# One-query attention over 8192 keys: VectorE turns the outputs for 64-byte stores, TensorE takes the value sum of two heads back first, and scores and softmax of a head run in one go

## The chip, the core and the metric

The kernel runs on one core of one Trainium2 chip. The metric is the device time of one execution in microseconds (us); the median of three runs of the kernel before is 326.26 us (326.13 to 326.35). A profile of one more execution, with the time of every instruction and DMA, stands beside it.

A core has five engines that run side by side and meet at semaphores: TensorE (PE in the profile; its weight loads are PEld), VectorE (DVE), ScalarE (ACT), GpSimd (POOL) and SyncE (SP). Here SP only issues DMAs; ACT issues three. A DMA issue is carried out in the order in which its engine comes to it, after the waits that stand ahead of it.

## What is computed

```python
B, H, Sq, Sk, D = 1, 16, 1, 8192, 256          # q, k, v in bf16
def reference(q, k, v):
    scale = q.shape[-1] ** -0.5
    scores = jnp.einsum("bhqd,bhkd->bhqk", q, k) * scale
    p = _softmax(scores, axis=-1)
    return jnp.einsum("bhqk,bhkd->bhqd", p, v)
```

For each of 16 heads one query row of 256 numbers meets 8192 keys, and the softmax of the 8192 scores weighs 8192 rows of values. A head's keys are 4 MB (4096 KB in the profile's rows) and so are its values: 134.2 MB in all, each byte used once. The output is 16 rows of 256 bf16 numbers, 8 KB.

## The kernel before

**Layout.** Partition p holds keys 64p to 64p+63 of a head, so a block of 64 keys of 256 numbers lies in each of the 128 partitions (`kbuf`, `vbuf`; two buffers of each, for even and odd heads). J is 64, the number of keys in a partition; j counts them.

**One head h** goes through these steps.

1. *Scores.* VectorE takes 48 of the 64 keys of each partition: 48 multiply-and-sum instructions (L189), each of which leaves one column of `S`. TensorE takes the other 16 (`NPE`), in four groups (`NG`) of four keys: it transposes a group (L292), ScalarE copies the transposed group from PSUM to `KT` (L392), and TensorE multiplies it with the query (L306). ScalarE then copies the 16 columns into `S` (L396, semaphore `sc`), and the last of VectorE's 48 instructions waits for that copy (L188). VectorE's last instruction raises `kd`.
2. *Maximum.* VectorE takes the maximum of `S` along each partition (L205, `m`), TensorE turns that column into a row (L226), VectorE takes its maximum (L171, `xmax`, result `g`), and TensorE spreads it over the partitions (L232, `bcast`).
3. *Exponentials.* ScalarE negates the maximum (L400) and takes the exponentials into `E`, with sums along each partition (L404). TensorE adds the sums up (L242, `total`), and VectorE takes the reciprocal (L176, `recips`).
4. *Value sum* (`pv`, L258). TensorE runs 128 matmuls of one column: the weights are a 128x128 block of `vbuf`, the moving column is one of `E`. Output number 2p+f of the head comes to partition p, column f (f is 0 or 1), because the weights are every second column of `vbuf`. ScalarE scales the two columns with the reciprocal into `o_col` (L416, `final`).

**Order on TensorE.** A loop over i has nine turns; turn i works on heads 2i and 2i+1, and on the value sums of heads 2i-2 and 2i-1. Written out for turn i: scores of 2i; value sum of 2i-2, and between its matmuls the maximum's turn (after 32 of 64 keys), the spreading (after 48) and the total (after 64) of head 2i-1; the maximum's turn of 2i, scores of 2i+1 with the spreading of 2i after the second group; value sum of 2i-1; total of 2i. Turn 0 has no value sums, turn 8 no scores; branches skip those parts.

**Order of the loads.** SP issues them from a list. From head 2 on it is: keys of h+2, values of h. Keys of h+2 wait for `kd` of head h (VectorE is done with the buffer), values of h wait for `pv` of head h-2. SP stands at each wait, so a late one holds back everything behind it. The values of head 14 come in two halves and those of head 15 in five pieces (`V_LATE`: from keys 0, 28, 46, 56 and 61), each with a semaphore of its own, so that TensorE can begin head 15's sum before its last piece is there.

**The end.** The outputs of heads 0 to 14 lie in `o_col`, 128 partitions by 30 columns. When TensorE is 46 keys into head 15's sum, it turns them with two matmuls against an identity (L274) into 15 rows of 256; ScalarE copies these to `o_row` (L470) and stores them in one DMA of 15 runs of 512 bytes (L472). Head 15's two columns are scaled by ScalarE (L416) and stored as they lie: 128 runs of 4 bytes (L475). ScalarE waits for both stores.

Of the kernel before, what the change touches and what calls it, by code (L numbers as in the profile page):

```python
# [14 lines left out]
V_LATE = {14: (0, 32), 15: (0, 28, 46, 56, 61)}  # L15
# [24 lines left out]
def bass_standalone__mha_softmax__decode_kernel(nc: bass.Bass, q: bass.AP, k: bass.AP, v: bass.AP, out: bass.AP):  # L40
# [28 lines left out]
    with contextlib.ExitStack() as ctx:  # L69
# [31 lines left out]
        o_col = sb("o_col", [P, H * NH], out.dtype)  # L101
        o_row = sb("o_row", [H - 1, D], out.dtype)
# [10 lines left out]
        for name in ("l", "rc", "pv", "fin", "ldq", "k0", "k0a", "k0b", "k1", "va0", "va1", "tr", "cp", "o"):  # L113
            sem(name)
# [8 lines left out]
        if True:  # L123

            @(lambda f: f(nc.sync))
            def _(sp):
                for kind, h, a, b, name in stream:
                    buf = (kbuf if kind == "k" else vbuf)[h % 2]
                    if h >= 2 and a == 0:
                        if kind == "k":  # L130
                            sp.wait_ge(sem("kd"), h)
                        else:
                            sp.wait_ge(sem("pv"), h + 1)
                    sp.dma_start(  # L134
                        buf[:, a * D : b * D], src(k if kind == "k" else v, h)[:, a * D : b * D]
                    ).then_inc(sem(name), 16)
                sp.nop()

            @(lambda f: f(nc.gpsimd))
            def _(pool):  # L140
# [18 lines left out]
                pool.memset(ones_row[:, :], 1.0).then_inc(sem("cf"), 1)  # L159
                pool.memset(ones_col[:, :], 1.0).then_inc(sem("cf"), 1)  # L160
# [7 lines left out]
            def _(dve):  # L168
# [37 lines left out]

                with dve.Fori(0, H // 2) as i:  # L207
# [12 lines left out]
                recips(last)  # L220

            @(lambda f: f(nc.tensor))
            def _(pe):
# [26 lines left out]
                def pv(h, waits, at):  # L250
# [3 lines left out]
                    for j in range(J):  # L254
                        for name, value in waits.get(j, ()):
                            pe.wait_ge(sem(name), value)
                        for hf in range(NH):
                            ins = pe.matmul(  # L258
                                acc[h.par][:, hf : hf + 1],
                                lhsT=vbuf[h.par][:, j * D + hf : (j + 1) * D : NH],  # L260
# [7 lines left out]
                        if j + 1 in at:  # L268
                            at[j + 1]()

                def rows():
                    pe.wait_ge(sem("fin"), H + 3)
                    for hf in range(NH):
                        ins = pe.matmul(  # L274
                            spe[0 : H - 1, hf : D : NH],
                            lhsT=o_col[:, hf : (H - 1) * NH : NH],
                            rhs=identb[:, :],
                            start=True,
                            stop=True,
                        )  # L280
                    ins.then_inc(sem("tr"), 1)
# [33 lines left out]
                def scores(t, before=None):  # L315
                    if before:
                        transpose_m(before)
                    for gi in range(NG):
                        ktrans(t, gi)
                        if gi >= 1:  # L320
                            kscore(t, gi - 1)
                        if gi == 1 and before:
                            bcast(before)
                    kscore(t, NG - 1)

# [31 lines left out]
                pe.wait_ge(sem("cf"), 4)  # L357
                with pe.Fori(0, H // 2 + 1) as i:
                    ev, od = _Step(0, i), _Step(1, i)
                    fin_turn = pe.snap((i // 8) * 16 + 16)  # L360
                    old = od.back(2)
                    with pe.If(i < H // 2):
                        scores(ev)
                    with pe.If(i > 0):
                        pv(
                            ev.back(2),
                            {V_LATE[14][n]: [(V_SEMS[0][n], fin_turn)] for n in range(1, len(V_SEMS[0]))},
                            {32: lambda: transpose_m(old), 48: lambda: bcast(old), 64: lambda: total(old)},
                        )
                    with pe.If(i < H // 2):  # L370
                        scores(od, before=ev)
                    with pe.If(i > 0):
                        waits = {V_LATE[15][n]: [(V_SEMS[1][n], fin_turn)] for n in range(1, len(V_SEMS[1]))}


                        def at_end():
                            with pe.If(i == H // 2):
                                rows()

                        pv(old, waits, {V_LATE[15][2]: at_end})  # L380
                    with pe.If(i < H // 2):
                        total(ev)

            @(lambda f: f(nc.scalar))
            def _(act):
# [58 lines left out]
                act.wait_ge(sem("cf"), 4)  # L444
                with act.Fori(0, H // 2) as i:
                    for c in (0, 1):
                        t = _Step(c, i)
                        for gi in range(NG):
                            evac(t, gi)
                        if c:  # L450
                            expo(t.back(1))
                        scopy(t)
                        act.wait_ge(sem("kd"), t.of(1, 1))
                        q_copy(_Step(c + 1, i), q_all[:, bass.ds(i * (2 * QW) + (c + 1) * QW, QW)])
                        with act.If(i > 0):
                            if c == 0:
                                expo(t.back(1))
                            else:
                                for d in (0, 1):
                                    at = nc.s_assert_within(  # L460
                                        (i - 1) * (2 * NH) + d * NH,
                                        0,
                                        (H - 1) * NH,
                                        skip_runtime_bounds_check_because="the branch is taken from turn 1 on",
                                    )
                                    final(t.back(3 - d), o_col[:, bass.ds(at, NH)])
                expo(_Step(H - 1))
# [4 lines left out]
                act.dma_start(out[0, 0 : H - 1, 0, :], o_row[:, :]).then_inc(sem("o"), 16)  # L472
                final(_Step(H - 1), o_col[:, (H - 1) * NH : H * NH])
                act.wait_ge(sem("fin"), H + 4)
                act.dma_start(  # L475
                    out[0, H - 1, 0, :].rearrange("(p f) -> p f", f=NH), o_col[:, (H - 1) * NH : H * NH]
                ).then_inc(sem("o"), 16)
                act.wait_ge(sem("o"), 32)
# [29 lines left out]
```

## Time and profile before

| | us |
|---|---|
| median of three runs | 326.26 |
| the profiled execution, its own time | 326.59 |
| span of its profile, first instruction to last | 325.1 |
| PE busy (3189 matmuls) | 168.6 |
| PEld busy | 143.9 |
| DVE busy | 274.8 |
| ACT busy | 91.1 |
| POOL busy | 1.6 |

The span leaves out 1.49 us of the profiled execution's own time. Busy times overlap and need not add up to the span. In a row of the timeline the columns are: start, duration, engine and line, operation, tiles written <- read, shapes, number of instructions merged into the row, and in brackets the idle time of the engine before it and what ended it. SPq and ACTq are issues of DMAs. In the list of waits the columns are: who waited, for whom, us in total, how often, the longest. In the list of DMA issues the last column is the time from the issue to the landing.

### The profile page before, as it was taken

To read this page: it belongs to the slowest core of one execution; us is meant where nothing else is said; L and a number is where in the kernel's file an instruction comes from. 1 tells how busy PE (TensorE), PEld (TensorE's weight loads), DVE (VectorE), ACT (ScalarE), POOL (GpSimd) and SP (SyncE) were. 2 spreads that over 40 slices of the span, in tenths; PEclk is the share of its full clock that TensorE was granted. 3 is DMA by queue.
4 is the path that set the end of the run, shared out by engine and by line. 5 is a ranking of instruction groups with operands and counts; after the bars stand their busy time and mean duration, and the time that the engine had idled before them with its cause. 6 is when DMAs were issued, how large, how long until landed. Compare 5 with 4: busy or idle time off the path is not lost.

```text
span 325.1 us, 8819 instructions
## 1 busy us (share of the span) xinstructions
PE 168.6 (52%) x3189; PEld 143.9 (44%) x3189; DVE 274.8 (85%) x1584; ACT 91.1 (28%) x173; POOL 1.6 (0%) x11
## 2 busy tenths in 40 slices
PE   4427280856467247643456454554646525675560
PEld 1326260755357235543335443444545424555550
DVE  3998999999999998897979979798897979979400
ACT  5435140425024140512306041250503305042010
POOL 1000000000000000000000000000000000000000
DMA  8999999999999999999999999999999999999970
GB/s 317 455 397 441 413 458 411 395 423 431 439 435 423 439 431 431 427 439 431 427 435 435 423 439 427 431 431 431 435 427 435 435 423 435 435 427 413 428 304 0
DMA packets 6116, 134.31 MB, mean 413 GB/s; under 512 B 831, under 2 KB 990, under 8 KB 1246
## 3 DMA queue, kind: packets, MB, share of 16 engines
q1 hardware_dynamic: 5904, 134.22, 96.5%
q8 instruction: 3, 0.05, 0.1%
q10 hardware_dynamic: 206, 0.02, 0.0%
q14 instruction: 3, 0.02, 0.0%
HBM read 134.23 MB, written 0.01 MB: 413 GB/s over the span
## 4 chain that ended last, share of the span: by engine, by line
DVE 50%; DMA 42%; issue 3%; PE 1%; SPq 1%; DVEq 0%; ACT 0%; ACTq 0%
DVE kbuf L189 47%; DMA kbuf<-in_k_dram 28%; DMA vbuf<-in_v_dram 14%; DVE S L189 2%; PE acc L258 1%; SPq L134 1%; DVE g L171 1%; DVE recip L176 0%; PE mx L226 0%; DVE m L205 0%; DVEq L181 0%; ACT o_col L416 0%; DVEq L207 0%; DVEq L180 0%; ACTq L415 0%
## 5 line engine op out<-in xcount | busy, mean ns | idle before, releaser
L189 DVE CUSTOM_DVE_ANT_0 kbuf<-kbuf,q_now 128x256 bf16<-128x256 bf16 x768 | 268.6, 414 | 28.4 <-DMA kbuf<-in_k_dram 27.4
L392 ACT ACTIVATE KT<-tp 128x1024 bf16<-128x1024 bf16 x64 | 63.8, 1022 | 98.6 <-PE tp L292 97.9
L292 PE MATMUL tp<-identb,kbuf 128*128 128x128 bf16 x512 | 62.8, 310 | 49.1 <-DMA kbuf<-in_k_dram 49.1
L258 PE MATMUL acc<-E,vbuf 128*128 128x1 bf16 x2048 | 60.4, 165 | 44.1 <-DMA vbuf<-in_v_dram 43.9
L258 PEld LDWEIGHTS acc<-E,vbuf 128*128 128x128 bf16 x2048 | 57.4, 104 | 49.6 <-DMA vbuf<-in_v_dram 46.2
L292 PEld LDWEIGHTS tp<-identb,kbuf 128*128 128x128 bf16 x512 | 50.7, 142 | 54.0 <-DMA kbuf<-in_k_dram 48.2
L189 DVE DVE_READ_ACCUMULATOR2_ANT S<- 128x1 f32 x768 | 58.8, 77 | 0.0
L306 PE MATMUL spe<-q_now,KT 128*128 128x1 bf16 x512 | 24.3, 169 | 16.7 <-ACT KT L392 15.9
L306 PEld LDWEIGHTS spe<-q_now,KT 128*128 128x128 bf16 x512 | 20.7, 108 | 26.4 <-ACT KT L392 21.6
L400 ACT ACTIVATE negb<-sm 128x1 f32<-128x1 f32 x16 | 2.7, 168 | 73.8 <-PE sm L232 73.8
L232 PE MATMUL sm<-g,ones_row 1*128 1x1 f32 x32 | 9.3, 356 | 21.3 <-DVE g L171 21.3
L232 PEld LDWEIGHTS sm<-g,ones_row 1*128 1x128 f32 x32 | 7.9, 304 | 22.0 <-DVE g L171 21.9
L226 PE MATMUL mx<-ident,m 128*1 128x128 f32 x32 | 9.4, 396 | 12.1 <-issue 6.2
L416 ACT ACTIVATE o_col<-acc,recip 128x2 f32 (+1 forms) x16 | 4.1, 254 | 39.8 <-PE acc L258 39.8
L242 PE MATMUL qps<-lsum,ones_col 128*128 128x1 f32 x32 | 9.1, 352 | 0.3 <-ACT E L404 0.3
L242 PEld LDWEIGHTS qps<-lsum,ones_col 128*128 128x128 f32 x32 | 8.0, 311 | 0.4 <-ACT E L404 0.4
L226 PEld LDWEIGHTS mx<-ident,m 128*1 128x1 f32 x32 | 1.4, 81 | 13.0 <-DVE m L205 6.6
L387 ACT ACTIVATE q_now<-q_all 128x258 bf16 x16 | 6.7, 418 | 0.1
L176 DVE RECIPROCAL recip<-qps 128x1 f32<-128x1 f32 x16 | 2.6, 165 | 4.2 <-PE qps L242 4.2
L171 DVE TENSOR_REDUCE g<-mx 1x1 f32<-1x128 f32 x16 | 4.4, 275 | 1.7 <-PE mx L226 1.7
L404 ACT ACTIVATE E<-S,negb 128x64 bf16<-128x64 f32 x16 | 5.6, 348 | 0.5
L348 PE MATMUL acc<-q_sb,identb 16*128 16x256 bf16 x16 | 4.3, 404 | 0.8 <-ACT q_all L439 0.8
(27 smaller groups left out, 21.1 us busy)
## 6 DMA issues: line engine op xcount, KB each, us to landing
kbuf<-in_k_dram SPq DMA_DIRECT2D x15, 4096.0 KB, 21.7
vbuf<-in_v_dram SPq DMA_DIRECT2D x12, 4096.0 KB, 31.1
vbuf<-in_v_dram SPq DMA_DIRECT2D x6, 2048.0 KB, 21.9
kbuf<-in_k_dram SPq DMA_DIRECT2D x2, 1024.0 KB, 5.9
kbuf<-in_k_dram SPq DMA_DIRECT2D x1, 2048.0 KB, 11.4
vbuf<-in_v_dram SPq DMA_DIRECT2D x1, 1792.0 KB, 10.4
vbuf<-in_v_dram SPq DMA_DIRECT2D x1, 1152.0 KB, 12.9
vbuf<-in_v_dram SPq DMA_DIRECT2D x1, 640.0 KB, 14.0
```

The costliest lines, as they stand in the source:

```text
L171: dve.tensor_reduce(g[0:1, h.par : h.par + 1], mx[0:1, 0:P], AX.X, ALU.max).then_inc(sem("g"), 1)
L189: ins = dve.tensor_tensor_reduce(out=buf[:, j * D : (j + 1) * D], in0=buf[:, j * D : (j + 1) * D], in1=q_now[h.par][:, 0:D], scale=SCALE, ...
L226: pe.matmul(mx[0:1, 0:P], lhsT=m[:, h.par : h.par + 1], rhs=ident[:, :], start=True, stop=True).then_inc(sem("mT"), 1)
L232: pe.matmul(sm[:, 0:1], lhsT=ones_row[0:1, 0:P], rhs=g[0:1, h.par : h.par + 1], start=True, stop=True,).then_inc(sem("bc"), 1)
L242: pe.matmul(qps[:, 0:1], lhsT=ones_col[:, 0:1].to_broadcast([P, P]), rhs=lsum[:, h.par : h.par + 1], start=True, stop=True,).then_inc(sem( ...
L258: ins = pe.matmul(acc[h.par][:, hf : hf + 1], lhsT=vbuf[h.par][:, j * D + hf : (j + 1) * D : NH], rhs=E[h.par][:, j : j + 1], start=(j == ...
L292: ins = pe.transpose(tp[gi % 2][:, b * D + hf * P : b * D + (hf + 1) * P], buf[:, j * D + hf * P : j * D + (hf + 1) * P], identb[:, :],)
L306: ins = pe.matmul(spe[:, c : c + 1], lhsT=KT[gi % 2][:, b * D + hf * P : b * D + (hf + 1) * P], rhs=q_now[h.par][:, D + hf : D + hf + 1], ...
L348: ins = pe.matmul(acc[pair % 2][:, (h % 2) * D : (h % 2 + 1) * D], lhsT=identb[0:H, h : h + 1].to_broadcast([H, P]), rhs=q_sb[:, :], start ...
L387: act.activation(out=q_now[h.par][:, :], in_=src_q, func=ACT.Copy).then_inc(sem("qb"), 1)
L392: act.activation(out=KT[gi % 2][:, :], in_=tp[gi % 2][:, :], func=ACT.Copy).then_inc(sem("kt"), 1)
L404: act.activation(out=E[h.par][:, :], in_=S[h.par][:, :], func=ACT.Exp, bias=negb[:, h.par : h.par + 1], scale=1.0, accum_out=lsum[:, h.par ...
```

## The change

Four things are changed together.

**Order on TensorE and ScalarE.** Turn i is now, for c = 0 and 1: value sum of head 2i-2+c, then scores of head 2i+c with the maximum's turn, the spreading and the total of the same head right behind them. ScalarE's part of a head follows suit: scaling of head t-2's output, the next query, the four copies, the copy into `S`, the exponentials of head t itself. On VectorE `xmax` of a head comes after the fourth, and `recips` after the twenty-first instruction of the next head, for even and odd heads alike.

**The values of head 14** come in one DMA, not in two halves.

**Column layout of the outputs.** The weights of the value sum are 128 neighbouring columns of `vbuf`, not every second: output number 128f+p comes to partition p, column f.

**Turning and storing.** TensorE's two turning matmuls and ScalarE's copy are gone. VectorE transposes `o_col` (128x32) in blocks of 32x32 into `o_row`, and ScalarE stores heads 0 to 14 in four DMAs, each of 30 runs of 64 bytes. Head 15's columns are scaled by VectorE into `z_col` (128x64, zeroed by GpSimd at the start, one live column in each block of 32), transposed into `z_row`, and stored by SP, which has issued all loads by then: 8 runs of 64 bytes. SP waits for all five stores. VectorE, TensorE and ScalarE wait at their start until GpSimd's two added memsets are done as well (`cf` reaches 6, not 4).

```diff
-V_LATE = {14: (0, 32), 15: (0, 28, 46, 56, 61)}
+V_LATE = {15: (0, 28, 46, 56, 61)}
+BLK = 32
...
+                sp.wait_ge(sem("tr"), 2)
+                sp.dma_start(
+                    out[0, H - 1, 0, :].rearrange("(f b x) -> b f x", f=NH, x=BLK),
+                    z_row[0:P:BLK, :].rearrange("b (f x) -> b f x", f=NH),
+                ).then_inc(sem("o"), 16)
+                sp.wait_ge(sem("o"), 16 * (P // BLK + 1))
...
-                    head(ev, {2: lambda: later(recips, ev.back(2)), 40: lambda: later(xmax, prev)})
-                    head(od, {2: lambda: later(recips, prev), 3: lambda: xmax(ev)})
+                    head(ev, {3: lambda: later(xmax, prev), 20: lambda: later(recips, prev)})
+                    head(od, {3: lambda: xmax(ev), 20: lambda: recips(ev)})
                 last = _Step(H - 1)
-                recips(last.back(1))
                 xmax(last)
                 recips(last)
+                dve.wait_ge(sem("fin"), H + 3)
+                dve.transpose(o_row[:, :], o_col[:, :]).then_inc(sem("tr"), 1)
+                dve.wait_ge(sem("rc"), last.of(1, 3))
+                dve.wait_ge(sem("pv"), last.of(1, 3))
+                dve.tensor_scalar(
+                    out=z_col[:, 0 : NH * BLK : BLK],
+                    in0=acc[last.par][:, 0:NH],
+                    scalar1=recip[:, last.par : last.par + 1],
...
+                dve.transpose(z_row[:, :], z_col[:, :]).then_inc(sem("tr"), 1)
...
-                                lhsT=vbuf[h.par][:, j * D + hf : (j + 1) * D : NH],
+                                lhsT=vbuf[h.par][:, j * D + hf * P : j * D + (hf + 1) * P],
...
+                def scores(t):
                     for gi in range(NG):
                         ktrans(t, gi)
                         if gi >= 1:
                             kscore(t, gi - 1)
                     kscore(t, NG - 1)
+                    transpose_m(t)
+                    bcast(t)
+                    total(t)
...
+                    for c, waits in (
+                        (0, {HALF: [(V_SEMS[0][1], 16)]}),
+                        (1, {V_LATE[15][n]: [(V_SEMS[1][n], fin_turn)] for n in range(1, len(V_SEMS[1]))}),
+                    ):
+                        with pe.If(i > 0):
+                            pv(_Step(c, i).back(2), waits)
+                        with pe.If(i < H // 2):
+                            scores(_Step(c, i))
...
                 final(_Step(H - 2), o_col[:, (H - 2) * NH : (H - 1) * NH])
                 act.wait_ge(sem("tr"), 1)
-                act.activation(out=o_row[:, :], in_=spe[0 : H - 1, 0:D], func=ACT.Copy).then_inc(sem("cp"), 1)
-                act.wait_ge(sem("cp"), 1)
-                act.dma_start(out[0, 0 : H - 1, 0, :], o_row[:, :]).then_inc(sem("o"), 16)
-                final(_Step(H - 1), o_col[:, (H - 1) * NH : H * NH])
-                act.wait_ge(sem("fin"), H + 4)
-                act.dma_start(
-                    out[0, H - 1, 0, :].rearrange("(p f) -> p f", f=NH), o_col[:, (H - 1) * NH : H * NH]
-                ).then_inc(sem("o"), 16)
-                act.wait_ge(sem("o"), 32)
+                rows = out.rearrange("b h s (f e) -> (b h s f) e", f=NH)
+                for b in range(0, P, BLK):
+                    act.dma_start(
+                        rows[0 : (H - 1) * NH, b : b + BLK], o_row[b : b + (H - 1) * NH, :]
+                    ).then_inc(sem("o"), 16)
```

On TensorE, before, this is the middle of a turn: after the scores of the even head 2i the skip of turn 0 (L364), the value sum of 2i-2 (L258), and between its matmuls the softmax steps of the odd head before (`mx` the maximum's turn, `sm` the spreading, `qps` the total).

```order
L364 COMPARE_AND_BRANCH
L252 ISA
L253 ISA
L258 MATMUL acc<-E,vbuf 128x1 x64
L226 MATMUL mx<-ident,m 1x128
L256 ISA
L258 MATMUL acc<-E,vbuf 128x1 x32
L232 MATMUL sm<-g,ones_row 128x1
L258 MATMUL acc<-E,vbuf 128x1 x32
L241 REGISTER_ALU
L242 MATMUL qps<-lsum,ones_col 128x1
```

On TensorE, after the change, the same place: the last score matmuls of the even head, its three softmax steps, and then the value sum of the odd head before.

```order
L316 MATMUL spe<-q_now,KT 128x1 x8
L249 REGISTER_ALU
L250 MATMUL mx<-ident,m 1x128
L256 MATMUL sm<-g,ones_row 128x1
L265 REGISTER_ALU
L266 MATMUL qps<-lsum,ones_col 128x1
L375 UNCONDITIONAL_BRANCH
L373 COMPARE_AND_BRANCH
L276 ISA
L277 ISA
L282 MATMUL acc<-E,vbuf 128x1 x56
```

The softmax steps have moved out of the value sum and stand, all three, between a head's scores and the value sum of the head before it; the scores of the next head come behind that value sum.

On ScalarE, before, this is the program's end: after the loop the exponentials of head 15, the scaling of head 14, the copy of the turned rows with their store, and the scaling and store of head 15.

```order
L445 COMPARE_AND_BRANCH
L400 ACTIVATE negb<-sm 128x1
L404 ACTIVATE E,lsum<-S,negb 128x64
L416 ACTIVATE o_col<-acc,recip 128x2
L470 ACTIVATE o_row<-spe 15x256
L472 DMA out_dram<-o_row 15x256
L416 ACTIVATE o_col<-acc,recip 128x2
L475 DMA out_dram<-o_col 128x2
```

On ScalarE, after the change, the last steps of the loop (copy into `S`, then the exponentials of the same head), its branch, and the program's end.

```order
L390 ACTIVATE S<-spe 128x16
L393 REGISTER_ALU
L394 ACTIVATE negb<-sm 128x1
L398 ACTIVATE E,lsum<-S,negb 128x64
L439 REGISTER_ALU
L439 COMPARE_AND_BRANCH
L410 ACTIVATE o_col<-acc,recip 128x2
L460 DMA out_dram<-o_row 30x32 x4
```

The exponentials have moved into the head's own step, the copy to `o_row` is gone, one store has become four, and head 15's scaling and store have left ScalarE for VectorE and SP.

More of the change, by code (lines that the diff above doesn't have):

```diff
@@ L267, in pv @@
                             ins.then_inc(sem("pv"), 1)
[L268 to L281, printed above, removed]
                 def ktrans(h, gi):
@@ L448, in _ @@
+                        q_copy(_Step(c + 1, i), q_all[:, bass.ds(i * (2 * QW) + (c + 1) * QW, QW)])
                         for gi in range(NG):
                             evac(t, gi)
-                        if c:
-                            expo(t.back(1))
                         scopy(t)
[L453 to L466, printed above, removed]
```

57 lines of the change are left out of this document (25 added, 32 removed).

## The prediction, made before the changed kernel was run

> **What bounds the kernel now.** I read the page first, then the windows (us; busy time of each engine; granted clock, DMA share, GB/s), then whom SP, the issuer of the loads, waits for.
>
> ```profile
> span 325.1 us, 8819 instructions
> PE 168.6 (52%) x3189; PEld 143.9 (44%) x3189; DVE 274.8 (85%) x1584; ACT 91.1 (28%) x173; POOL 1.6 (0%) x11
> DMA  8999999999999999999999999999999999999970
> ...
> 151.00:190.00 39.00, 20.52 (x399) 17.90 (x399) 34.45 (x199) 10.55 (x20) 0.00 (x0) 1.00 1.00 432
> ...
> SPq L134 <- DVE S L189: 250.0, 14, 19.2
> SPq L134 <- PE acc L258: 33.4, 2, 17.6
> ```
>
> The DMA engines are busy from the first slice to the last but one; in the middle their share is 1.00. The last slice (317 to 325 us) is empty of DMA and, as the end below shows, of everything else. SP waits for VectorE, but that costs nothing while the queue is full. So 314 us are loading, and the last 8 are something else. One turn in the middle:
>
> ```profile
> 167.89 0.33 SPq L134 DMA_DIRECT2D kbuf<-in_k_dram  x1
> ...
> 170.38 1.89 PE L292 MATMUL tp<-identb,kbuf 128*128 128x128 bf16 x16 [1.62 <-DMA kbuf<-in_k_dram]
> ...
> 180.10 3.58 PE L258 MATMUL acc<-E,vbuf 128*128 128x1 bf16 x128 [3.16 <-DMA vbuf<-in_v_dram]
> ...
> 187.46 0.33 SPq L134 DMA_DIRECT2D kbuf<-in_k_dram  x1
> ...
> 189.81 1.89 PE L292 MATMUL tp<-identb,kbuf 128*128 128x128 bf16 x16 [5.71 <-DMA kbuf<-in_k_dram]
> ```
>
> Keys land at 170.38, values at 180.10, the next keys at 189.81: 9.7 us for 4 MB, 19.43 us a head. VectorE needs 274.8/16 = 17.2 us a head, so the loads set the pace. The end:
>
> ```profile
> 296.67 3.57 PE L258 MATMUL acc<-E,vbuf 128*128 128x1 bf16 x128 [3.15 <-DMA vbuf<-in_v_dram]
> ...
> 306.47 1.01 PE L258 MATMUL acc<-E,vbuf 128*128 128x1 bf16 x32 [1.56 <-DMA vbuf<-in_v_dram]
> ...
> 308.80 0.57 PE L242 MATMUL qps<-lsum,ones_col 128*128 128x1 f32 x2
> ...
> 310.77 1.65 PE L258 MATMUL acc<-E,vbuf 128*128 128x1 bf16 x56 [1.40 <-DMA vbuf<-in_v_dram]
> 313.55 1.12 PE L258 MATMUL acc<-E,vbuf 128*128 128x1 bf16 x36 [1.13 <-DMA vbuf<-in_v_dram]
> ...
> 315.12 1.59 PE L258 MATMUL acc<-E,vbuf 128*128 128x1 bf16 x36
> ...
> 315.63 0.58 ACTq L472 DMA_DIRECT2D out_dram<-o_row  x1
> 316.81 0.26 ACT L416 ACTIVATE o_col<-acc,recip 128x2 bf16<-128x2 f32 x1 [1.21 <-PE acc L258]
> 317.10 0.37 ACTq L475 DMA_DIRECT2D out_dram<-o_col  x1
> ...
> out_dram<-o_row ACTq DMA_DIRECT2D x1, 7.5 KB, 1.3
> out_dram<-o_col ACTq DMA_DIRECT2D x1, 0.5 KB, 8.0
> ```
>
> TensorE follows the last pieces of values as they land and is done at 315.12 + 1.59 = 316.71. The store of 15 runs of 512 bytes lands in 1.3 us, that of 128 runs of 4 bytes in 8.0 us: 317.10 + 8.0 is the span's end. A fifteenth of the bytes takes six times as long, so runs, not bytes, are paid for.
>
> **The new order in the middle: cost nothing.** The value sum now stands ahead of the next head's scores. Values of t-2 land 9.7 us after keys of t, so the scores of t start later than now, and VectorE's last instruction waits for them. The length of the scores, from the one place where they run alone:
>
> ```profile
> 39.02 1.89 PE L292 MATMUL tp<-identb,kbuf 128*128 128x128 bf16 x16 [5.67 <-DMA kbuf<-in_k_dram]
> ...
> 44.68 0.38 PE L306 MATMUL spe<-q_now,KT 128*128 128x1 bf16 x8 [0.69 <-ACT KT L392]
> ...
> 45.09 0.18 ACT L396 ACTIVATE S<-spe 128x16 f32<-128x16 f32 x1 [0.47 <-PE spe L306]
> ```
>
> 45.09 + 0.18 - 39.02 = 6.25 us, ScalarE's copies within. In the quoted turn: values land at 180.1, sum to 183.7, scores to 189.9, VectorE's last instruction some 0.4, then SP issues the next keys at 190.4 instead of 187.46. Behind SP's wait stand those keys and the values after them. The queue holds until the values in flight land, 180.1 + 19.43 = 199.5. Less 1.3 us to get going (an estimate: the small store's whole time) that leaves a margin of 7.8 us. This is the cover; once the chain is longer, every us costs about one per head. VectorE idles up to 3 us more a head and works just behind the landing instead of ahead of it. The value wait of SP (`pv`) is met at 183.7, before the key wait: nothing. The loop kd, softmax (3.6, below), sum 3.6, scores 6.25, last instruction 0.4 is 13.9 us, under 19.4, so it doesn't bind either.
>
> **The new order at the end: +1.0 us.** Scores of head 15 now wait for the value sum of 13 (ends 296.67 + 3.57 = 300.24), and both remaining sums wait for head 15's softmax. Its steps, from VectorE's last instruction of a head:
>
> ```profile
> 303.60 0.41 DVE L189 CUSTOM_DVE_ANT_0 kbuf<-kbuf,q_now 128x256 bf16<-128x256 bf16 x1
> ...
> 304.32 0.58 PE L226 MATMUL mx<-ident,m 128*1 128x128 f32 x2 [0.89 <-DVE m L205]
> 304.95 0.28 DVE L171 TENSOR_REDUCE g<-mx 1x1 f32<-1x128 f32 x1 [0.49 <-PE mx L226]
> ...
> 56.45 0.27 DVE L171 TENSOR_REDUCE g<-mx 1x1 f32<-1x128 f32 x1
> 56.78 0.58 PE L232 MATMUL sm<-g,ones_row 1*128 1x1 f32 x2 [8.44 <-DVE g L171]
> ...
> 58.17 0.57 PE L242 MATMUL qps<-lsum,ones_col 128*128 128x1 f32 x2
> ```
>
> Scores end at 300.24 + 6.25 = 306.5; now the last instruction starts at 303.60. To the start of L171 1.35, to the spreading 0.33, to the total 1.39, the total 0.57: 310.1. With 0.2 for the loop's branch the sum of 14 runs from 310.3 (its values landed at 306.47, so that their coming in one DMA costs nothing) to 313.9. With 0.2 for the skipped scores, the sum of 15 runs from 314.1 to 317.7; the pieces land ahead of it (the second at 313.5, the rest by 316.4, now's end less the six last matmuls). 317.7 instead of 316.71. Bounds: 0 (the data's own limit) to +1.8, because of the weights, now neighbouring columns:
>
> ```profile
> L258 PE MATMUL acc<-E,vbuf 128*128 128x1 bf16 x2048 | 60.4, 165 | 44.1 <-DMA vbuf<-in_v_dram 43.9
> ...
> L306 PE MATMUL spe<-q_now,KT 128*128 128x1 bf16 x512 | 24.3, 169 | 16.7 <-ACT KT L392 15.9
> ```
>
> L306 loads such weights already: eight in 0.38 us, (380 - 169)/7 = 30 ns apart, against (3580 - 165)/127 = 27 ns for L258. I take the same 27; at 30 the two sums are 0.8 longer.
>
> **The end itself: -6.3 us.** VectorE's scaling follows the last matmul by 0.1, as ScalarE's does now: 317.8. The trace has no VectorE scaling or transpose of this kind; the nearest row is the 0.28 of L171, bounds 0.1 and 0.5 each; I take 0.28 twice and a hand-over: issue by SP at 318.45 instead of 317.10. Its 8 runs of 64 bytes land in 1.3 us at best (o_row) and 8.0 at worst (o_col). I take 1.3, since 8 runs are nearer to 15 than to 128. End 319.8, so **-5.3 us** with the 1.0 from above (317.10 + 8.0 = 325.1 against 318.45 + 1.3). The four row stores start once VectorE has turned heads 0 to 14, 313.9 + 0.1 + 0.26 + 0.28 = 314.6; four issues of 0.58 (L472) put the last at 316.3, landed by 317.7: beside the last sum. The removed turning matmuls and copy lay in front of 315.63, off the path: nothing. GpSimd's two memsets come on top of 1.6 us for eleven instructions:
>
> ```profile
> 5.65 0.42 DVE L189 CUSTOM_DVE_ANT_0 kbuf<-kbuf,q_now 128x256 bf16<-128x256 bf16 x1 [5.65 <-DMA kbuf<-in_k_dram]
> ...
> 8.06 1.09 PE L348 MATMUL acc<-q_sb,identb 16*128 16x256 bf16 x4 [0.20 <-ACT q_all L439]
> 13.13 1.87 PE L292 MATMUL tp<-identb,kbuf 128*128 128x128 bf16 x16 [3.98 <-DMA kbuf<-in_k_dram]
> ...
> 22.36 0.33 SPq L134 DMA_DIRECT2D kbuf<-in_k_dram  x1
> ...
> 25.34 0.59 PE L226 MATMUL mx<-ident,m 128*1 128x128 f32 x2 [6.20 <-issue]
> ```
>
> VectorE waits until 5.65 for keys anyway: nothing. TensorE's first skip over a value sum cost 6.20 us in which it waited for nothing shown. Now that skip comes at 9.2, before the scores of head 0: they start at 15.4 instead of 13.13 and end at 21.7, just before VectorE's last instruction (22.36 less 0.4). Nothing, by 0.3 us.
>
> **Rivals.** *Small stores are paid by the run.* (8.0 - 1.3)/128 = 52 ns a run; 120 row runs take 6.3 us: 314.6 + 1.3 + 6.3 + 0.4 for the last eight = 322.6, **323.8** as a measured time. For it: o_col. Against: its runs shared 512 bytes, sixteen runs to each 64, while no two of the new ones share 64 bytes. The Trainium skill, DMA: Bandwidth & Descriptors, section Specifications, puts the line at 512 B: below it the engine reads, modifies and writes. By that rule 64 bytes fare like 4, and the time is this rival's; the 1.3 of the 512-byte runs agrees with the rule, and nothing here shows 64.
>
> *The last store is slow whatever its runs.* If what takes 8.0 us is a store's landing after the loads, not its runs, the end is 318.45 + 8.0 = 326.5, **327.6**, slower. It decides from a landing of 7.3 us on (8.0, less the later issue of 1.35, plus 0.65 or 0.2%). Against: o_row's 1.3, taken while the last loads landed.
>
> *The queue runs dry early.* VectorE begins heads late at first:
>
> ```profile
> 59.17 0.33 SPq L134 DMA_DIRECT2D kbuf<-in_k_dram  x1
> ...
> 73.25 1.89 PE L292 MATMUL tp<-identb,kbuf 128*128 128x128 bf16 x16 [2.74 <-DMA kbuf<-in_k_dram]
> ```
>
> Keys issued at 59.17 landed at 73.25; their transfer began by 63.5, so issue may slip to 62.2. The first visit of each value sum may cost 6.2 us like the skip. Head 1 leaves VectorE at 22.4 + 17.2 = 39.6; softmax 3.6, stall 6.2, sum 3.6, scores 6.25 and 0.4 put the issue at 59.7. It holds by 2.5; a second stall in the scores, and the same for head 3, would cost 1 to 3 us: **322 to 324**.
>
> *Skips cost 6.2 us in the last turn too.* The one between the last two sums would put the end at 325.8: **327.0**. Against: the same skip now lies between 308.80 + 0.57 = 309.4 and 310.77, where values landed; so it takes 1.4 us at most. The Trainium skill, Runtime: NRT & Kernel Launch, section Instruction fetch mechanics, says that a taken branch out of the fetched window waits for a fetch; turn 0 agrees, the last turn does not.
>
> **How the numbers follow.** The profiled execution took 326.59, 1.49 beyond its span; the median is 326.26, so I take the difference from the median: 326.26 - 5.3 = 320.9. Chances: forecast 0.64 (its own range 319.8 to 322.3: tail 0 to 1.8, VectorE's two steps, landing to 2.0), runs 0.12, dry queue 0.10, slow last store 0.09, skips 0.05. The range reaches over the first three, 319.8 to 324.2. These are faster by over 0.2% (0.65 us, about what a measurement can tell): 0.86. Of the other 0.14, 0.04 fall within 0.2% and 0.10 beyond.
>
> **What would show it.** SP's issue of keys some 3 us later in each turn, DMA share still 1.00 in the middle; TensorE done near 317.7; the row stores landed before the last issue; o_col's 8.0 replaced by under 2. It is wrong if a window before 300 us has a DMA share under 1.00, or a 64-byte store takes over 3 us.

## The result and the profile after

The changed kernel took 320.96 us (median of four runs, 320.66 to 321.17), beside 326.31 us for the kernel before on the same chip (four runs, 326.13 to 326.6). The ratio is 0.9835, with a 95% interval of 0.9818 to 0.9852: 5.3 us faster, as forecast (320.9). The profiled execution took 321.17, 1.27 beyond its span.

The page after, first its busy times, then its slices of DMA:

```profile
span 319.9 us, 8825 instructions
...
PE 166.6 (52%) x3187; PEld 141.6 (44%) x3187; DVE 276.0 (86%) x1587; ACT 91.8 (29%) x171; POOL 1.7 (1%) x13
...
DMA  8999999999999999999999999999999999999993
```

The work is the same, and so is the loading: only the empty time behind the last loads is gone. The last slice is shorter and no longer empty. The window of one turn in the middle (us, length, busy time of PE, PEld, DVE, ACT and POOL, granted clock, DMA share, GB/s), and whom SP waits for:

```profile
151.00:190.00 39.00, 20.23 (x396) 17.51 (x396) 34.46 (x199) 10.81 (x21) 0.00 (x0) 1.00 1.00 432
```

```profile
SPq L137 <- DVE S L200: 253.7, 14, 18.9
SPq L137 <- PE acc L282: 31.1, 2, 19.1
SPq L141 <- DVE z_row L244: 15.5, 1, 15.5
SPq L146 <- DMA out_dram<-z_row: 1.0, 1, 1.0
```

The DMA share is 1.00 at 432 GB/s, both as before. SP still waits most for VectorE. The last line, 1.0 us for the landing of head 15, and the 0.68 us of its issue, below, are what the 8.0 of `o_col` has become. The timeline of a turn:

```profile
180.26 3.57 PE L282 MATMUL acc<-E,vbuf 128*128 128x1 bf16 x128 [5.50 <-DMA vbuf<-in_v_dram]
...
183.70 1.87 PE L302 MATMUL tp<-identb,kbuf 128*128 128x128 bf16 x16
...
189.95 0.43 DVE L200 CUSTOM_DVE_ANT_0 kbuf<-kbuf,q_now 128x256 bf16<-128x256 bf16 x1 [2.21 <-ACT S L390]
...
190.41 0.33 SPq L137 DMA_DIRECT2D kbuf<-in_k_dram  x1
...
194.15 0.59 PE L266 MATMUL qps<-lsum,ones_col 128*128 128x1 f32 x2 [0.73 <-ACT E L398]
```

The values still land at 180.26 (180.10 before), their sum now stands in front of the scores, VectorE's last instruction has the new wait of 2.21 us, and SP issues the next keys at 190.41 where it had issued them at 187.46. The timeline of the end:

```profile
296.84 3.57 PE L282 MATMUL acc<-E,vbuf 128*128 128x1 bf16 x128 [5.51 <-DMA vbuf<-in_v_dram]
...
306.32 0.18 ACT L390 ACTIVATE S<-spe 128x16 f32<-128x16 f32 x1 [0.47 <-PE spe L316]
...
309.55 0.58 PE L266 MATMUL qps<-lsum,ones_col 128*128 128x1 f32 x2 [0.73 <-ACT E L398]
...
310.36 7.13 PE L282 MATMUL acc<-E,vbuf 128*128 128x1 bf16 x256 [0.23 <-issue]
...
314.33 0.21 DVE L233 STREAM_TRANSPOSE o_row<-o_col 128x32 bf16<-128x32 bf16 x1 [3.99 <-ACT o_col L410]
314.57 1.85 ACTq L460 DMA_DIRECT2D out_dram<-o_row  x4
317.61 0.23 DVE L236 TENSOR_SCALAR z_col<-acc,recip 128x2 bf16<-128x2 f32 x1 [3.07 <-PE acc L282]
317.87 0.25 DVE L244 STREAM_TRANSPOSE z_row<-z_col 128x64 bf16<-128x64 bf16 x1
318.15 0.68 SPq L141 DMA_DIRECT2D out_dram<-z_row  x1
```

TensorE no longer stops for pieces of values: the sums of heads 14 and 15 are one row of 256 matmuls without a gap, done at 310.36 + 7.13 = 317.49 (316.71 before). From there it is 0.66 us to the last issue, and 0.68 + 1.0 from that to its landing: 319.83, the span's end.

### The profile page after: what moved, and what is told of

The parts are those of the page before. It is cut to its first block, busy times and chain, and to the rows that moved or that the text cites. A ratio compares the mean times of both kernels' runs of the same rounds, so it can differ in the third digit from the quotient of the medians.

```text
span 319.9 us, 8825 instructions
## 1 busy us (share of the span) xinstructions
PE 166.6 (52%) x3187; PEld 141.6 (44%) x3187; DVE 276.0 (86%) x1587; ACT 91.8 (29%) x171; POOL 1.7 (1%) x13
## 4 chain that ended last, share of the span: by engine, by line
DMA 59%; PE 18%; DVE 12%; ACT 5%; issue 4%; SPq 1%; DVEq 0%; ACTq 0%
DMA vbuf<-in_v_dram 52%; DVE kbuf L200 11%; PE acc L282 9%; DMA kbuf<-in_k_dram 7%; PE tp L302 6%; ACT KT L386 5%; PE spe L316 2%; SPq L137 1%; ACT S L390 0%; DVE S L200 0%; PE sm L256 0%; PE qps L266 0%; DVE g L182 0%; PE mx L250 0%; ACT E L398 0%
## 5 line engine op out<-in xcount | busy, mean ns | idle before, releaser
L200 DVE CUSTOM_DVE_ANT_0 kbuf<-kbuf,q_now 128x256 bf16<-128x256 bf16 x768 | 269.4, 410 | 31.8 <-ACT S L390 21.2
L282 PE MATMUL acc<-E,vbuf 128*128 128x1 bf16 x2048 | 57.1, 166 | 60.4 <-DMA vbuf<-in_v_dram 60.0
L282 PEld LDWEIGHTS acc<-E,vbuf 128*128 128x128 bf16 x2048 | 56.0, 104 | 61.7 <-DMA vbuf<-in_v_dram 61.0
L200 DVE DVE_READ_ACCUMULATOR2_ANT S<- 128x1 f32 x768 | 55.8, 73 | 0.0
L390 ACT ACTIVATE S<-spe 128x16 f32<-128x16 f32 x16 | 2.9, 183 | 7.5 <-PE spe L316 7.5
## 6 DMA issues: line engine op xcount, KB each, us to landing
vbuf<-in_v_dram SPq DMA_DIRECT2D x1, 640.0 KB, 13.9
```

The lines of the kernel that those rows point to most:

```text
L200: ins = dve.tensor_tensor_reduce(out=buf[:, j * D : (j + 1) * D], in0=buf[:, j * D : (j + 1) * D], in1=q_now[h.par][:, 0:D], scale=SCALE, ...
L282: ins = pe.matmul(acc[h.par][:, hf : hf + 1], lhsT=vbuf[h.par][:, j * D + hf * P : j * D + (hf + 1) * P], rhs=E[h.par][:, j : j + 1], star ...
```

## The experiments

Two questions were to be told apart. How much of the 5.3 us is the end, and what does the new order cost? And why is the old last store slow: is it paid by its 128 runs, by their crowding in 512 bytes, or because it is the last? Eleven kernels ran, in three groups, each beside the kernel before (326.25, 326.7 and 326.28 us).

| kernel | us (median) | ratio to before, interval |
|---|---|---|
| after, again | 320.95 | 0.9835 [0.9822, 0.9849] |
| old order, new end | 320.61 | 0.9822 [0.9809, 0.9835] |
| old order, last head's store alone new | 320.48 | 0.9817 [0.9804, 0.9831] |
| new order, old end | 327.26 | 1.0028 [1.0019, 1.0037] |
| 60 idle transposes a head | 321.86 | 0.9863 [0.9838, 0.9888] |
| last store on two queues | 320.75 | 0.9831 [0.9818, 0.9845] |

The five others are single runs, and are read by a landing or by far larger differences. Between profiles of one kernel the loads land some tenths sooner or later (the sum of head 13 begins at 296.84 in one profile of the changed kernel and at 296.59 in that of its second run here), so the ends of two profiles are compared from a landing that both have: this sum begins as its values land, at 296.67 in the profile before and at 296.84 after. From there TensorE is done after 20.04 us before (316.71) and after 20.65 in the changed kernel (317.49).

**The changed kernel again**, as the reference for the others of its group:

> The changed kernel once more, beside the other three of this call: 320.96 as measured, within 0.3.

It took 320.95 (320.71 to 321.02).

**The old order with the new end.** The hunks of the change for weights, turning and stores on the kernel before; its order and the halves of head 14 stay. Against the kernel after, on TensorE:

```diff
-                        with pe.If(i > 0):
-                            pv(_Step(c, i).back(2), waits)
-                        with pe.If(i < H // 2):
-                            scores(_Step(c, i))
+                    with pe.If(i < H // 2):
+                        scores(ev)
+                    with pe.If(i > 0):
+                        pv(ev.back(2), ..., {32: lambda: transpose_m(old), 48: lambda: bcast(old), 64: lambda: total(old)})
+                    with pe.If(i < H // 2):
+                        scores(od, before=ev)
+                    with pe.If(i > 0):
+                        pv(old, waits, {})
+                    with pe.If(i < H // 2):
+                        total(ev)
```

> The orders of before on TensorE, ScalarE and VectorE and the two halves of head 14's values, with the new column layout, turning and stores. Theory (the stores bring the gain, the order costs about 1 at the end and nothing in the middle): TensorE is done at 316.7 as before, SP issues the last store 0.7 later, it lands 1.7 after that as it does in the changed kernel: span 319.1, time 320.2 to 320.4, that is 0.6 to 0.9 below the changed kernel. Rival (the new order brings part of the gain): the time lies above the changed kernel's 321.

It took 320.61 (320.3 to 320.76). The timeline of its end:

```profile
296.93 3.57 PE L283 MATMUL acc<-E,vbuf 128*128 128x1 bf16 x128 [3.16 <-DMA vbuf<-in_v_dram]
...
315.43 1.57 PE L283 MATMUL acc<-E,vbuf 128*128 128x1 bf16 x36 [0.48 <-DMA vbuf<-in_v_dram]
...
317.12 0.23 DVE L237 TENSOR_SCALAR z_col<-acc,recip 128x2 bf16<-128x2 f32 x1 [7.19 <-PE acc L283]
...
317.66 0.68 SPq L141 DMA_DIRECT2D out_dram<-z_row  x1
```

The new end by itself gives 326.25 - 320.61 = 5.6 us, all of the gain and 0.3 more. The new order costs that 0.3 (320.95 - 320.61); the intervals overlap, so by the medians its sign is shown only together with the kernel that has the old end, below. The expectation was lower (a larger cost of the order). In this profile TensorE waits for values until 315.43 and is done at 317.00, 0.3 later than the kernel before (316.71) with the same order, because the loads land that much later in it: the sum of head 13 begins at 296.93, and 20.07 us pass from there, as before (20.04). Against the 20.65 of the changed kernel the order costs 0.6 us by the profiles. Why loads land later in one profile than in another was not settled.

**The old order, and only the last head's store new.** As the one before, but heads 0 to 14 are turned by TensorE, copied by ScalarE and stored in one DMA of 512-byte runs:

```diff
-                rows = out.rearrange("b h s (f e) -> (b h s f) e", f=NH)
-                for b in range(0, P, BLK):
-                    act.dma_start(
-                        rows[0 : (H - 1) * NH, b : b + BLK], o_row[b : b + (H - 1) * NH, :]
-                    ).then_inc(sem("o"), 16)
+                act.activation(out=o_row[:, :], in_=spe[0 : H - 1, 0:D], func=ACT.Copy).then_inc(sem("cp"), 1)
+                act.wait_ge(sem("cp"), 1)
+                act.dma_start(out[0, 0 : H - 1, 0, :], o_row[:, :]).then_inc(sem("o"), 16)
```

> As the run before, but heads 0 to 14 are turned by TensorE, copied by ScalarE and stored in one DMA of 512-byte runs, as in the kernel before; only head 15 goes through VectorE and SP. Theory (the row stores are beside the value sum, only the last store counts): the same time as the run before within 0.3, 320.2 to 320.5. Rival (the row stores' 120 runs of 64 bytes hold the last store up): 0.5 or more below the run before.

It took 320.48 (320.03 to 320.78): not told apart from 320.61. The four row stores with their 120 runs of 64 bytes lie beside the path, and the whole gain is in how head 15 is turned and stored.

**The new order with the old end.** The order of the change; weights, turning matmuls, copy and stores of the kernel before:

```diff
-                            pv(_Step(c, i).back(2), waits)
+                            pv(_Step(c, i).back(2), waits, {V_LATE[15][2]: at_end} if c else {})
...
+                act.dma_start(
+                    out[0, H - 1, 0, :].rearrange("(p f) -> p f", f=NH), o_col[:, (H - 1) * NH : H * NH]
+                ).then_inc(sem("o"), 16)
```

> The new orders on the engines and head 14's values in one DMA, with the column layout, the turning on TensorE and the two stores of before. Theory (the order costs 0.8 to 1.4 at the end, the two turning matmuls now lying inside the last sum, and nothing else): 327.1 to 327.7, slower than before. Rival (the order saves time in the middle): at or below the 326.3 of before.

It took 327.26 (326.63 to 327.78, eleven runs), 1.0 us more than before, and the interval of the ratio lies above 1. The timeline of its end, and its list of DMA issues (last column: us from issue to landing):

```profile
296.56 3.58 PE L258 MATMUL acc<-E,vbuf 128*128 128x1 bf16 x128 [5.52 <-DMA vbuf<-in_v_dram]
...
310.04 6.17 PE L258 MATMUL acc<-E,vbuf 128*128 128x1 bf16 x220 [0.18 <-issue]
316.14 0.59 PE L274 MATMUL spe<-identb,o_col 128*15 128x128 bf16 x2
316.66 1.12 PE L258 MATMUL acc<-E,vbuf 128*128 128x1 bf16 x36
317.88 0.26 ACT L404 ACTIVATE o_col<-acc,recip 128x2 bf16<-128x2 f32 x1 [0.74 <-PE acc L258]
318.17 0.36 ACTq L457 DMA_DIRECT2D out_dram<-o_col  x1
```

```profile
out_dram<-o_col ACTq DMA_DIRECT2D x1, 0.5 KB, 8.1
```

Alone, the new order is a loss. From the start of the sum of head 13 TensorE is done after 21.2 us (317.78 - 296.56), 1.2 more than before. Of that 0.5 is the two turning matmuls (from 316.14 to 316.66): in the old order they fell into a wait for values, here they stand in a sum that waits for nothing. The rest, 0.7, is about the 0.6 that the order costs with the new end, which takes these matmuls out. By the medians the order is worth +1.0 with the old end and +0.3 with the new one, and the new end is worth -5.6 in the old order and -6.3 (327.26 - 320.95) in the new one.

**Idle transposes in front of the scores**, in turns 2 to 6, to make SP's issue of the keys later and see where the cover ends (60 and 110 of them, the count in the third line):

```diff
+                        with pe.If(i > 1):
+                            with pe.If(i < H // 2 - 1):
+                                for _ in range(60):
+                                    pe.transpose(tp[0][:, 0:P], identb[:, :], identb[:, :])
                         with pe.If(i < H // 2):
                             scores(_Step(c, i))
```

> The changed kernel with 60 idle transposes (some 5.8 us) between value sum and scores in turns 2 to 6, heads 4 to 13. SP issues keys 10.3 us after values land; with the pad 16.1, against 18.1 at which the queue would run dry by my estimate. Theory (a margin of 7.8 us covers the new order): no change, 321 within 0.5, SP's issues 5.8 us later. Rival (the margin is used up or smaller than 5 us): each of ten heads pays up to 5.8 us, 330 to 380.

With 60 it took 321.86 (321.45 to 322.61). The timeline of one head, and a window of four heads' loads:

```profile
183.20 5.60 PE L378 MATMUL tp<-identb 128*128 128x128 bf16 x60
...
194.35 0.33 SPq L137 DMA_DIRECT2D kbuf<-in_k_dram  x1
```

```profile
120.00:200.00 80.00, 57.38 (x1064) 52.08 (x1065) 70.76 (x409) 21.07 (x40) 0.00 (x0) 0.67 1.01 432
```

From the end of the value sum to SP's issue of keys it is 194.35 - 183.20 = 11.15 us, in the changed kernel 190.41 - 183.70 = 6.71. The keys come 4.4 later, and the loads still run at 432 GB/s. The time is 0.9 above the changed kernel's, a little more than the 0.5 that was allowed (0.5 when each is held against the kernel before in its own group, and the intervals of the ratios overlap); had each of the ten padded heads passed on the 4.4, it would be 44. The loads are not late in this profile: the sum of head 13 begins at 296.33, in the changed kernel at 296.84. What is late is the end: the sum of head 14 begins at 310.59, 0.2 later, and 0.4 pass between it and that of head 15, where the changed kernel has no gap. So of the margin of 7.8 us that was forecast to be left, some 4 at least are there.

> The same with 110 (some 10.7 us): 21.0 us after the landing, 2.9 over the margin, ten heads: about 350 by the theory, between 340 and 360. Rival (the issue of the keys isn't what the queue waits for): 321 as without.

With 110 it took 342.86, inside what the theory gave, but for another reason. Its timeline of one head, and the same window:

```profile
208.16 0.33 SPq L137 DMA_DIRECT2D kbuf<-in_k_dram  x1
...
212.69 3.57 PE L282 MATMUL acc<-E,vbuf 128*128 128x1 bf16 x128 [0.21 <-issue]
216.13 7.75 PE L378 MATMUL tp<-identb 128*128 128x128 bf16 x110
...
229.44 0.33 SPq L137 DMA_DIRECT2D kbuf<-in_k_dram  x1
```

```profile
120.00:200.00 80.00, 61.59 (x1159) 56.96 (x1158) 65.00 (x375) 19.16 (x39) 0.00 (x0) 0.72 0.95 396
```

A head takes 21.3 us from issue to issue (208.16 to 229.44), more than the 19.4 of its loads, and the value sum waits for no values any more (0.21, where it was 5.50): the loop of softmax, sum, transposes and scores is itself longer than the loads. So this run tells nothing of where the queue would run dry, and the upper half of the 7.8 us is not tested.

**Why the old last store is slow.** Four forms of the kernel before with its last store, still in runs of 4 bytes, spread out or cut: 64, 16 or 8 bytes from one run to the next (head 15's numbers then lie over other heads' output, so the store waits for the first one), and 16 runs instead of 128. The spacing X is 32, 8 or 4 numbers:

```diff
+                act.wait_ge(sem("o"), 16)
                 act.dma_start(
-                    out[0, H - 1, 0, :].rearrange("(p f) -> p f", f=NH), o_col[:, (H - 1) * NH : H * NH]
+                    out.rearrange("b h s d -> (b h s d)")[0 : P * X].rearrange("(p x) -> p x", x=X)[:, 0:NH],
+                    o_col[:, (H - 1) * NH : H * NH],
                 ).then_inc(sem("o"), 16)
```

> The kernel before, with its last store of 128 runs of 4 bytes spread over the whole output, 64 bytes from run to run (it overwrites parts of other heads' rows, which are stored and landed first). If 8.0 us is what runs cost that share 64 bytes with fifteen others, each run now has its 64 bytes to itself: landing in 1.3 to 2.5 us, time 320 to 321.5. If every short run costs 52 ns wherever it lies, landing in 8.0 us and 326.3 as before.

> The same with 16 bytes from run to run, four runs to each 64 bytes. Sharing: 1.3 + 6.7 x 4/16 = 3.0 us to landing, time 321 to 322. By the run: 8.0 us and 326.3.

> The kernel before with its last store's 128 runs of 4 bytes 8 bytes apart, eight to each 64 bytes (over other heads' rows, stored before). If the landing grows with the number of runs that share 64 bytes, it lies between the 2.2 us of four and the 8.0 of sixteen, on their line at 2.2 + 5.8 x 4/12 = 4.1 us: 3.5 to 4.7, time 322 to 323.2. If sharing is harmless until the runs touch one another, 2.5 us or less.

```diff
-                    out[0, H - 1, 0, :].rearrange("(p f) -> p f", f=NH), o_col[:, (H - 1) * NH : H * NH]
+                    out[0, H - 1, 0, 0 : 16 * NH].rearrange("(p f) -> p f", f=NH),
+                    o_col[0:16, (H - 1) * NH : H * NH],
```

> The kernel before with its last store cut to 16 partitions: 16 runs of 4 bytes in one stretch of 64 bytes (the other 448 bytes of head 15's row are not written). If runs that share 64 bytes wait for one another, stretch by stretch, the one stretch takes as long as eight side by side: 6 to 8 us to landing, time 324.5 to 326.3. If all short runs of the store stand in one line wherever they fall, 16 take 1.3 + 16 x 0.05 = 2.1 us: time 320.5.

Their lists of DMA issues, the last store of each: 64 apart, 16 apart, 8 apart, and 16 runs.

```profile
out_dram<-o_col ACTq DMA_DIRECT2D x1, 0.5 KB, 1.4
```

```profile
out_dram<-o_col ACTq DMA_DIRECT2D x1, 0.5 KB, 2.2
```

```profile
out_dram<-o_col ACTq DMA_DIRECT2D x1, 0.5 KB, 3.1
```

```profile
out_dram<-o_col ACTq DMA_DIRECT2D x1, 0.1 KB, 1.3
```

128 runs of 4 bytes land in 1.4 us when each has 64 bytes to itself. So neither their number nor their size nor their place behind the loads makes the old store slow by itself; how close they lie does: 1.4, 2.2, 3.1 and 8.0 us for 1, 4, 8 and 16 runs in 64 bytes. What sharing was expected to give was too high in between (3.0 for the 2.2, 3.5 to 4.7 for the 3.1). And the last kernel has 16 runs in one 64-byte stretch too and takes 1.3, against the 6 to 8 that sharing of 64 bytes alone gave, so the number of runs in 64 bytes does not decide by itself. Counted in 512 bytes, these five stores have 8 runs (64 apart), 16 (the cut store), 32, 64 and 128, for 1.4, 1.3, 2.2, 3.1 and 8.0 us, in order but for a tenth. Whether it is the number in such a longer stretch, several runs of one DMA engine in one stretch, or eight stretches at once, stays open: no kernel here separates them.

By the packet records of the traces the wait lies behind the DMA engines, not in them. The last packet of the store ends 1.06 us after the issue in the kernel before (318.16), and as soon with the runs 64, 16 and 8 bytes apart. Of the 8.0 us some 6.9 pass with no packet of any DMA moving, until the last part of the store is reported as landed.

The times were 321.56 us (64 apart), 321.04 (16), 321.85 (8) and 319.82 (16 runs). The first lies above the second, and just above the 320 to 321.5 expected, although its store lands sooner: the loads land late in that run, the sum of head 13 beginning at 298.24. The third and the fourth lie below what sharing gave, as their landings do.

**The last store on two queues.** The one with only the last store new, with half of head 15 issued by SP and half by ScalarE:

```diff
-                    out[0, H - 1, 0, :].rearrange("(f b x) -> b f x", f=NH, x=BLK),
-                    z_row[0:P:BLK, :].rearrange("b (f x) -> b f x", f=NH),
+                    out[0, H - 1, 0, 0:P].rearrange("(b x) -> b x", x=BLK), z_row[0:P:BLK, 0:BLK]
...
+                act.wait_ge(sem("tr"), 2)
+                act.dma_start(
+                    out[0, H - 1, 0, P:D].rearrange("(b x) -> b x", x=BLK), z_row[0:P:BLK, BLK : 2 * BLK]
+                ).then_inc(sem("o"), 16)
```

> As the run with the old order and only the last head's store changed, with that store split over SP and ACT, four runs of 64 bytes each. SP's issue of the one store took 0.68 us and 1.7 to landing; two plain ones take 0.35 to 0.6 and about 1.4: 320.2, 0.2 to 0.3 below the 320.48 of one store. Rival (the fixed time of a store is all there is): 320.5.

It took 320.75 (320.58 to 320.85). The issues in its timeline:

```profile
317.43 0.63 SPq L141 DMA_DIRECT2D out_dram<-z_row  x1
...
317.43 0.61 ACTq L496 DMA_DIRECT2D out_dram<-z_row  x1
```

Half the runs take 0.6 us to issue, about as all did (0.68): nothing is gained, and the 0.2 to 0.3 expected did not come. No kernel of these beats the changed one by more than the intervals hold; the three with the old order and the new last store lie 0.2 to 0.5 us below it.

## Why the prediction was right

**What bounds the kernel** held: DMA share 1.00 and 432 GB/s in the middle, before and after, and little gained or lost ahead of 300 us: the sum of head 13 begins at 296.84, before at 296.67.

**The new order in the middle, nothing.** Forecast: SP's issue at 190.4, VectorE idle up to 3 us more a head, DMA share still 1.00. Measured: 190.41, 2.21 and 1.00. Of the margin of 7.8 us the 60 transposes showed that some 4 at least exist. The loop without them was put at 13.9 us: it is 194.15 + 0.59 - 180.26 = 14.5 up to the total, from where the next sum could start. The forecast counted the last instruction's 0.4 twice, since its 3.6 for the softmax begin with that instruction; without it the sum is 13.5. The 1.0 that was missed lies in VectorE's maximum of the row (`xmax`), which now waits behind the first four instructions of VectorE's next head. The loop is still 4.9 under the loads' 19.4.

**The new order at the end, +1.0.** Step by step, forecast and profile: scores of head 15 done at 306.5 and 306.50; the sums from 310.3 and 310.36; TensorE done at 317.7 and 317.49. The loop's branch cost 0.23, forecast 0.2; the skip between the two sums cost nothing that the row of 256 matmuls shows, forecast 0.2. The weights in neighbouring columns, bounded at 27 and 30 ns, came to (7130 - 166)/255 = 27. So the path was right and the size too large. Counted from the start of the sum of head 13, the forecast has TensorE done after 21.0 us (317.7 - 296.67), the profile after 20.65, the kernel before after 20.04: the order costs 0.6, not 1.0, by the medians 0.3 with the new end. The skip's 0.2 is one part of the difference, tenths in the scores and sums the rest. (317.49 - 316.71 = 0.8 holds 0.2 of loads that landed later.)

**The end itself, -6.3.** VectorE's scaling came at 317.61 (forecast 317.8), the two steps took 0.23 and 0.25 (0.28 each, bounded by 0.1 and 0.5), and SP issued at 318.15 (318.45). The landing was the mis-sized term: 0.68 + 1.0 = 1.7 us instead of 1.3: the issue takes 0.68, where `o_row`'s took 0.58, and the landing behind the issue 1.0, where `o_row`'s was 1.3 - 0.58 = 0.7. From TensorE's last matmul to the span's end it is 2.4 us (319.9 - 317.49), before 8.4: -6.0, not -6.3. That the sum comes out at 319.83 against 319.8 is luck to the tenths: the landing 0.4 longer and the loads 0.2 later make up for the cheaper order and the earlier issue. That the landing is nearer to 1.3 than to 8.0 was chosen because 8 runs are nearer to 15 than to 128. The choice was right and its reason wrong, as was the reading that runs, not bytes, are paid for: 128 runs, given room, land in 1.4. Between kernels, by the medians, the end gave 5.6 us in the old order and 6.3 in the new.

**The row stores** were issued from 314.57 (forecast 314.6), the last of the four from 316.0 (316.3), and the wait that ends the kernel is put down to the last store, not to them; the version without them takes the same time. GpSimd's memsets cost nothing: VectorE's wait at the start is for keys as before, and POOL is busy for 1.7 us.

**Turn 0.** The timeline of its TensorE after:

```profile
14.59 1.86 PE L302 MATMUL tp<-identb,kbuf 128*128 128x128 bf16 x16 [5.53 <-DMA kbuf<-in_k_dram]
...
34.53 1.89 PE L302 MATMUL tp<-identb,kbuf 128*128 128x128 bf16 x16 [6.73 <-issue]
...
45.83 3.57 PE L282 MATMUL acc<-E,vbuf 128*128 128x1 bf16 x128 [0.21 <-issue]
...
58.97 0.33 SPq L137 DMA_DIRECT2D kbuf<-in_k_dram  x1
```

The scores of head 0 began at 14.59 instead of 13.13 (forecast 15.4), and the second skip, which the forecast of that turn did not count, cost 6.73 us with nothing in front of it that the profile shows, as the first skip before. Neither matters: the keys that were issued at 59.17 before are issued at 58.97.

**The rivals.** *Small stores are paid by the run* fell: 120 runs of 64 bytes beside the path, and 128 of 4 bytes in 1.4 us. The Trainium skill, DMA: Bandwidth & Descriptors, section Specifications, has transfers under 512 B read, modified and written. Here 64-byte runs behaved like 512-byte ones but for some tenths, and 4-byte runs too when spread: the trace does not agree with the time that the rival drew from this rule. Whether these runs were read and modified, no run here shows. *The last store is slow whatever its runs* fell by the same landing. *The queue runs dry early* did not come: the first visit of a value sum cost 0.21 us, not 6.2, and the issue at 58.97 lies ahead of the 59.7 that was feared. *Skips cost 6.2 us in the last turn too* fell by the row of 256 matmuls. The Trainium skill, Runtime: NRT & Kernel Launch, section Instruction fetch mechanics, has a taken branch out of the fetched window wait for a fetch: turn 0 agrees (6.73), the loop's branch at the end (0.23) and the last skip do not show it.

## What to carry to other kernels

Where a kernel is bound by loading, look at what lies behind the last load: a term there is paid in full, while an issue 3 us later in every turn cost nothing that the profile shows as long as the queue is filled ahead. A small last store is read by how its runs lie to each other, not by their number alone: few long runs, by a transpose on an idle engine if need be (8 of 64 bytes landed in 1.7 us), or short ones with room between them (1.4), rather than 128 short ones side by side (8.0). Work that was free because it fell into a wait (the two turning matmuls) costs its length when a new order takes the wait away, so such edits belong together and are summed together. Before the ends of two profiles are compared, count both from a landing that they share: a difference of some tenths may be the loads'.

## What was not expected of the hardware

A store of 128 runs of 4 bytes landed in 8.0 us when the runs touch, and in 3.1, 2.2 and 1.4 when they begin 8, 16 and 64 bytes apart; 16 touching runs landed in 1.3. All packets of these stores had ended 1.0 to 1.1 us after the issue.

The granted clock in the records does not say how fast TensorE ran here. In the kernel with 110 idle transposes it is 0.72 in the window above, in the changed kernel 1.00, and yet the same transposes were shorter with it. The groups by line of the changed kernel, and of that with 110:

```profile
L302 PE MATMUL tp<-identb,kbuf 128*128 128x128 bf16 x512 | 62.4, 310 | 12.3 <-issue 6.7
```

```profile
L302 PE MATMUL tp<-identb,kbuf 128*128 128x128 bf16 x512 | 46.3, 253 | 15.1 <-issue 8.7 <-DMA kbuf<-in_k_dram 6.2
```

One of these takes 253 ns instead of 310, and 110 idle ones follow each other at 7.75/110 = 70 ns, where the sixteen at 183.70 above do so at (1870 - 310)/15 = 104. Sixty of them moved SP's issue by 4.4 us and not by their own 5.6, because the transposes of the scores behind them ran faster too: the first sixteen took 1.06 us instead of 1.87. And with the transposes of the kernel before unchanged, the profile with its last store 64 apart has a mean granted clock of 0.537 and 308 ns for one of them, that of the kernel before 1.00 and 310.
